# Fp32 transformer block on one core: low parts of w2 subtracted on GpSimd in most of the first phase, and a new order of the opening

## The chip, the cores and the metric

The kernel runs on one core of one Trainium2 chip. The metric is the device time of one execution in microseconds (us), lower is better. A run's time is compared with that of the kernel before.

## The reference

The input x has 2048 tokens of 576 values, all in fp32. The output is the sum of x, a local attention and a relu MLP, both fed with the same normalised x:

```python
xn = (x - mean(x)) / sqrt(var(x) + 1e-5)            # by token
q, k, v = split(xn @ wqkv)                          # 32 heads of 18
# each token sees itself and 7 earlier ones: offsets 0, 2, 4, ... 14
logits = einsum("bhsd,bhswd->bhsw", q, kg) * 18**-0.5   # masked before the start
attn = softmax(logits)
A = einsum("bhsw,bhswd->bhsd", attn, vg) @ wo       # wo 576 x 576
B = maximum(xn @ w1, 0) @ w2                        # 576 -> 4608 -> 576
out = x + A + B
```

## The kernel before

**Split in two.** Each fp32 operand of a matmul is held as a high part (rounded to the short form fp32r) and a low part (the rest), and a product is made of three: high x high, high x low, low x high. `hi_lo` makes the parts: ACT rounds (L395), then DVE subtracts (L398) or, with `by_pool`, GpSimd does (L401; GpSimd is called POOL). The products with w1 and wqkv are regrouped as in Strassen's method into seven products, P1 to P7, each 7 matmuls into one bank of PSUM (`bk`, `bkA`, `pm`); sums of weights (`ts`, `wset`) and of x (`xs`) are formed by DVE, and partial results are carried in the tiles `sn`, to which DVE adds a bank (`sn<-bk`, L398). Only then may PE write that bank again.

**Phases, sets, groups.** The offsets are even, so even and odd tokens are independent: the kernel does the 1024 even ones, then the odd ones, in two phases. A phase goes through 25 sets of weights: 18 F sets (256 of the 4608 hidden values each, numbered m = 0 to 17 and 18 to 35) and 7 Q sets (256 columns of wqkv). For an F set the hidden values go to `hb` (ACT's relu and a low part by DVE, L819), and are multiplied with that group's 256 rows of w2, tiles `w2t`, two of 128x576 a group, into the two accumulators `po`. `w2_make` fetches w2 from a copy that GpSimd's DMAs (L588, each behind a one-element copy L587 that paces it) have made in the order of use (`w2c`, in the first phase; the other weights have such copies too), and splits it.

**Attention.** Four units a phase, 8 heads each, on DVE: for 8 blocks of tokens products q x k (L1299) and their sums (L1302), a mask by GpSimd (L1305), the softmax (L1311 to L1326), products with v (L1331) and three levels of sums (L1338), then a transpose of the result (L1344). SP, the queue of most DMAs, writes it out (L1351, L1359); for the last unit of a phase it reads back 16 columns of each head group (L1365), which DVE transposes (L1369, `turn16`). Group 17's output product with wo needs all that; L786 and L791 load the rows of wo for it.

**What sets the order.** A planner, class `Order`, runs while the program is written out. It keeps a clock for each engine, queues of operations with due times and estimated durations, and `back`, a list of DVE operations of the attention (added by `later`) that fill DVE's gaps. An operation takes its place in its engine's stream when the planner's clock says that it is ready and nothing more urgent is. An engine then runs its stream strictly in order. At group 16 of a phase all that is left in `back` is forced out (`wo_plan`).

**The opening.** The list `OPEN` gives PE's order until the seven-product form starts: T transposes of x, R its last 64 rows, F and Q products with the first F set and the first Q set (Q001: the first with the Q set), O products with w2, K starts of copies, B, W, S, M others. Ahead of it stand loads: x of the first blocks in `x_first`, the first sets in the order `RAWS`, whose four members C11 to C22 are 256 rows by 128 columns and whose member `None` is the last 64 rows. `normalise` of a block is: statistics (`bn_stats`, L433), mean and variance (`bn_aggr`, L440, L441) on DVE, the root on GpSimd (L442, L445), and the scaling by ACT (L453, with `by_act`) or DVE (L458). Before the opening PE runs warm-up matmuls (L385).

Of the kernel before, what the change touches and what calls it, by code (L numbers as in the profile page):

```python
# [31 lines left out]
WARM = 38  # L32
PADS = (16, 16, 32, 32)
OPEN = """
T2 K2 B0 W0 R2 B1 T3 Q001 R3 Q000 T4 F010 F011 R4 T5 O0101 R5 O0100 T6 K3
Q011 S0 R6 O0110 F100 T7 O0111 Q010 R7 S1 F101 O1000 F110 K4 F111 O1010
Q100 M2 O1001 O1011 W1 Q111 O1100 O1101 O1111 O1110 Q110 Q101
""".split()

S2, S4, S3, S1 = range(4)  # L40
T1, B11, T3, B21, B22, T2, T4 = range(7)
B12 = T3
C11, C12, C21, C22 = range(4)
ROWS = (0, 288)
R3 = 96
# [3 lines left out]
FAR = 1e9  # L49
# [15 lines left out]
class Order:  # L65
# [120 lines left out]
        return op  # L186

    def later(self, fn, n, after=(), lag=0.0):
        op = Op(DVE, n / 960.0 + 0.068, fn, after, FAR, lag)
        self.back.append(op)  # L190
        return op

# [60 lines left out]
def tile_body(ctx: ExitStack, tc: tile.TileContext, x, wqkv, wo, w1, w2, out):  # L253
# [172 lines left out]
    def normalise(i, src, after, slack, by_act=False, alloc=True):  # L426

        z = {}

        def sums():  # L430
            z["st"] = smp.tile([P, 2, 6], F32, name="bst", bufs=4)
            for h in range(2):
                nc.vector.bn_stats(z["st"][:, h, :], src()[:, h * D2 : (h + 1) * D2])  # L433

        def rest():
            v = MV[0]
            MV.append(MV.pop(0))
            z["mv"] = mv = v[:, 0:2]
            z["r"] = r = v[:, 2:3]
            nc.vector.bn_aggr(mv, z["st"])  # L440
            nc.vector.tensor_scalar(mv[:, 1:2], mv[:, 1:2], EPS, None, op0=ALU.add)  # L441
            nc.gpsimd.tensor_tensor(r, mv[:, 1:2], mhalf, op=ALU.pow)  # L442
            if by_act:
                z["nm"] = nm = v[:, 3:4]
                nc.gpsimd.tensor_scalar(nm, mv[:, 0:1], r, -1.0, op0=ALU.mult, op1=ALU.mult)  # L445

        a = dve(sums, D + 200, after, slack)
        b = dve(rest, 310, [a], slack + 0.5, lag=1.1 if by_act else 0.8)

        def one():  # L450
            if alloc:
                xn_alloc(i)
            nc.scalar.activation(XN[i], src(), AF.Identity, bias=z["nm"], scale=z["r"])  # L453

        def two():
            if alloc:
                xn_alloc(i)
            nc.vector.tensor_scalar(XN[i], src(), z["mv"][:, 0:1], z["r"], op0=ALU.subtract, op1=ALU.mult)  # L458

        def fours():  # L460
            src = XN[i].rearrange("p (q c) -> p q c", q=2)[:, :, 2 * P : 2 * P + DH]
            nc.gpsimd.tensor_copy(XF[0][:, i % 2], src[:, :, None, :].to_broadcast([P, 2, 4, DH]))

        if by_act:
            MEANS[i] = b
            a = act(one, D + 200, [b], slack + 1.0)
        else:
            a = dve(two, D // 2 + 100, [b], slack + 1.0)
        NORMED[i] = a
        before, XUSED[i] = XFREE[i % 2], stub()  # L470
        XFREE[i % 2] = XUSED[i]
        FOURS[i] = o_.gp(fours, 256, [a, before], slack + 2.0)

    FOURS, XF, XUSED, XFREE = {}, [None], {}, [None, None]

# [295 lines left out]
    def w2_make(m, f, after=()):  # L771
        W2[m, f] = w = w2p.tile([P, 2, D], F32R, name="w2t")
        g = send(lambda: nc.sync.dma_start(f32(w[:, 1]), W2C[m % NP][f * P : (f + 1) * P]), 295, [*kept["w2", m % NP], *after], 4.0)
        W2OK[m, f] = hi_lo(w[:, 0], w[:, 1], f32(w[:, 1]), D, [g], (7 if SETS[SF[m] - 1][1] == "Q" else 24 if NP <= m < NP + 3 else 12) + 2 * f)

    WO, WOOK = {}, {}

# [814 lines left out]
        XLAST[i] = max(HALVES[i], key=lambda z: z.end)  # L1592
    ST0 = [stp[b].tile([P, 2, 2, P], F32, name=f"stg{b}") for b in range(3)]
    nc.gpsimd.memset(ST0[2][R3:P], 0.0)
    RAWS = ((C11, 0, 0), (C21, 1, 0), (C12, 0, 1), (C22, 1, 1), (None, 0, 0))
    def by_pool_now(fn, kb):
        fn()
        o_.clk[GP_] += 0.6
        z = Op(GP_, 0.0, None, (), 0.0)
        z.end = o_.clk[GP_] + 2.4 + kb / 60.0  # L1600
        o_.dma += kb / 300.0
        return z

    STOF = {C11: ST0[0][:, 0], C21: ST0[0][:, 1], C12: ST0[1][:, 0], C22: ST0[1][:, 1]}
    SETOK[0], SETREST = {}, {}
    first = []
    for s_, hf, f in RAWS:
        if s_ is None:
            got = [
                by_pool_now(lambda: nc.gpsimd.dma_start(  # L1610
                    ST0[2][y * DH : (y + 1) * DH].rearrange("p v f c -> p v (f c)"),
                    last_rows(w1[:, 0 : 2 * P])), 64)
                for y in range(3)
            ]
        else:
            got = [send(lambda: nc.sync.dma_start(
                STOF[s_], w1[ROWS[hf] : ROWS[hf] + 256, f * P : (f + 1) * P].rearrange("(k p) c -> p k c", p=P)), 128)]
        first.append((s_, got))
# [46 lines left out]
    fours_home()  # L1665
    o_.clk[PE] = 7.5
    normalise(0, lambda: X[0], [XLAST[0]], 0, by_act=True)
    normalise(1, lambda: X[1], [XLAST[1]], 1)
    def norm1():
        NORM1.end = NORMED[1].end  # L1670

# [11 lines left out]
    for z, (s_, got) in enumerate(first):  # L1683
        after, behind = [*got, NORMED[0] if z else None], [NORMED[1] if z else None]
        if s_ is None:
            first_rest(0, ST0[2].rearrange("p v f c -> p (v f) c"), after, 3 + z, behind)
        else:
            SETOK[0][s_] = hi_lo(
                wset(0)[0][:, s_, 0:2], wset(0)[1][:, s_], STOF[s_], 256, after, 3 + z, behind, z > 1,
            )  # L1690
    for z in SETOK[0].values():
        z += SETREST[0]
# [143 lines left out]
```

## Time and profile before

Three runs: 1115.68 to 1116.13 us, median 1115.89. The profiled execution:

| | us |
|---|---|
| time of that execution | 1115.5 |
| its span in the trace | 1113.7 |
| PE (TensorE) busy | 1095.4 (98%) |
| DVE (VectorE) busy | 916.1 (82%) |
| ACT (ScalarE) busy | 759.2 (68%) |
| POOL (GpSimd) busy | 214.9 (19%) |

PE is the matmul engine, PEld its weight loads; their clock is granted by a throttle (1.00 is full speed). A row of a group reads: line, engine, operation, output<-inputs, sizes, count | busy us in total, mean ns of one | idle time of the engine ahead of it, and what ended most of it. A row of a timeline reads: start, duration, engine, line, operation, names, sizes, count [idle ahead <- what ended it]. All times count from the span's start. Names are those of the tiles; `pr` and `qo` are the attention's products and results, `xa`, `xr` the normalised x and its last rows.

### The profile page before, as it was taken

The numbers are of one execution on the slowest core, as the hardware profiler recorded it, in microseconds if no ns is written. First come the engines' busy times: TensorE is split into PE (matmuls) and PEld (weight loads), VectorE is DVE, ScalarE is ACT, GpSimd is POOL, SyncE is SP. The second block draws the span as 40 slices with busy tenths as digits, with TensorE's granted clock in tenths as the row PEclk, the third lists the DMA queues.
The fourth block names the chain that finished last, engine by engine and source line by source line (L and its number), as shares of the span: only waits on it lengthen the run. The fifth ranks groups of instructions, "written<-read, shape, count | busy, mean of one in ns | idle before, by whom it ended". The sixth has DMA issues, their size and how long they took to land.

```text
span 1113.7 us, 23965 instructions
## 1 busy us (share of the span) xinstructions
PE 1095.4 (98%) x8971; PEld 1091.8 (98%) x8971; DVE 916.1 (82%) x1722; ACT 759.2 (68%) x1575; POOL 214.9 (19%) x427
## 2 busy tenths in 40 slices
PE   7999999999999999979999999999999999999998
PEld 7999999999999999979999999999999999999998
DVE  6966999998999889975795689998999998997540
ACT  6856676567777767756695655666567776766774
POOL 6232473332752253310220000000000000000000
PEclk9999999999999999999999999999999999999999
DMA  6689788884894455345363864646535416223312
GB/s 187 191 203 218 182 204 236 214 212 135 257 229 130 124 153 168 105 96 141 109 183 83 205 145 91 160 112 138 140 104 139 123 44 158 84 63 74 104 51 85
DMA packets 357012, 160.93 MB, mean 144 GB/s; under 512 B 211200, under 2 KB 335552, under 8 KB 355664
## 3 DMA queue, kind: packets, MB, share of 16 engines
q1 hardware_dynamic: 349392, 135.81, 48.0%
q0 software_dynamic: 7344, 23.29, 7.1%
q8 instruction: 70, 1.15, 0.4%
q10 hardware_dynamic: 160, 0.30, 0.1%
q14 instruction: 46, 0.38, 0.1%
HBM read 126.62 MB, written 55.41 MB: 163 GB/s over the span
## 4 chain that ended last, share of the span: by engine, by line
PE 86%; DVE 6%; DMA 3%; ACT 2%; SPq 1%; issue 1%; POOL 0%; DVEq 0%; ACTq 0%; POOLq 0%
PE po L404 41%; PE bk L404 26%; PE pm L404 12%; PE bkA L404 6%; DMA x<-in_x 1%; DVE pr L1338 1%; DVE xa L398 1%; DMA kk<-qd 1%; DVE wset L398 1%; DVE pr L1331 1%; DVE xs L398 1%; SPq L859 1%; DVE hb L819 0%; DVE ts L398 0%; DMA qo<-in_w 0%
## 5 line engine op out<-in xcount | busy, mean ns | idle before, releaser
L404 PE MATMUL po<-w2t,hb 128*128 128x256 f32 (+1 forms) x3456 | 504.4, 292 | 0.0
L404 PEld LDWEIGHTS po<-w2t,hb 128*128 128x128 f32 x3456 | 463.6, 188 | 0.3 <-DVE hb L819 0.3
L395 ACT ACTIVATE x<-po 128x576 f32<-128x576 f32 x286 | 186.3, 651 | 224.3 <-PE po L404 223.5
L404 PE MATMUL bk<-xs,wset 128*128 128x256 f32 (+1 forms) x1584 | 222.4, 277 | 0.3 <-ACT bkA L395 0.2
L404 PEld LDWEIGHTS bk<-xs,wset 128*128 128x128 f32 (+1 forms) x1584 | 202.6, 186 | 0.8 <-ACT bkA L395 0.4
L404 PE MATMUL bk<-xa,wset 128*128 128x256 f32 (+1 forms) x1116 | 193.5, 279 | 6.5 <-DVE sn L398 6.4
L395 ACT ACTIVATE po<-x 128x576 f32<-128x576 f32 x286 | 187.1, 655 | 6.0 <-DVE x L398 0.2
L404 PEld LDWEIGHTS bk<-xa,wset 128*128 128x128 f32 (+1 forms) x1116 | 159.6, 188 | 7.4 <-DVE sn L398 7.1
L587 POOL COPY spare<-hb 1x1 f32<-1x1 f32 x175 | 87.8, 501 | 236.4 <-ACT hb L395 236.1
L404 PE MATMUL pm<-xs,wset 128*128 128x256 f32 (+1 forms) x720 | 102.0, 277 | 0.0
L404 PE MATMUL pm<-xa,wset 128*128 128x256 f32 (+1 forms) x552 | 94.5, 278 | 1.7 <-POOL wset L401 1.2
L404 PEld LDWEIGHTS pm<-xs,wset 128*128 128x128 f32 (+1 forms) x720 | 92.0, 187 | 0.1
L398 DVE TENSOR_TENSOR sn<-bk,sn 128x256 f32<-128x256 f32 (+1 forms) x132 | 55.0, 418 | 44.2 <-PE bk L404 21.9
L404 PE MATMUL bkA<-xa,wset 128*128 128x256 f32 (+1 forms) x636 | 89.8, 278 | 0.0
L1305 POOL TENSOR_SCALAR_AFFINE_SELECT lg<-lg 1x512 f32<-1x512 f32 x8 | 9.8, 1224 | 411.3 <-DVE lg L1302 411.3
L1299 DVE TENSOR_TENSOR pr<-qo,kk 128x1152 f32<-128x1152 f32 x64 | 85.2, 1344 | 3.7 <-DMA qo<-qd 3.4
L1302 DVE TENSOR_REDUCE lg<-pr 128x64 f32<-128x1152 f32 x64 | 85.3, 1342 | 0.4
L1331 DVE TENSOR_TENSOR pr<-lg,v 128x1152 f32<-128x1152 f32 x64 | 85.4, 1348 | 0.1
L395 ACT ACTIVATE hb<-sn 128x256 fp32r<-128x256 f32 x140 | 57.6, 414 | 39.8 <-DVE sn L398 39.0
L404 PEld LDWEIGHTS bkA<-xa,wset 128*128 128x128 f32 (+1 forms) x636 | 82.9, 187 | 0.2 <-ACT bkA L395 0.2
L404 PEld LDWEIGHTS pm<-xa,wset 128*128 128x128 f32 (+1 forms) x552 | 77.8, 187 | 2.3 <-POOL wset L401 1.6
L1338 DVE TENSOR_TENSOR pr<-pr 128x288 f32<-128x288 f32 (+1 forms) x128 | 70.8, 599 | 0.0
(162 smaller groups left out, 1480.2 us busy)
## 6 DMA issues: line engine op xcount, KB each, us to landing
w2t<-w2c SPq DMA_DIRECT2D x70, 288.0 KB, 3.6
wset<-rwd SPq DMA_DIRECT2D x48, 336.0 KB, 4.1
qd<-stg SPq DMA_DIRECT2D x216, 64.0 KB, 2.6
wset<-w1c SPq DMA_DIRECT2D x105, 128.0 KB, 2.9
w2c<-in_w POOLq DMA_DIRECT2D x68, 144.0 KB, 3.7
rwd<-kk SPq DMA_DIRECT2D x18, 448.0 KB, 4.4
w1c<-in_w POOLq DMA_DIRECT2D x51, 128.0 KB, 3.9
out<-x SPq DMA_DIRECT2D x16, 288.0 KB, 2.2
```

The source lines that it names most:

```text
L395: nc.scalar.activation(o, i, func)
L398: nc.vector.tensor_tensor(o, a, b, op=op)
L404: nc.tensor.matmul(o, l, r, start=start, stop=stop, skip_group_check=True)
L587: nc.gpsimd.tensor_copy(spare[0:1], f32(LATEST[-1])[0:1, 0:1])
L859: lambda: nc.sync.dma_start(dst.rearrange("i (b r) c -> r (i b) c", r=32), z[32 * a : 32 * (a + 1)].rearrange("r j (z c) -> r (j z) c", c=32),
L1299: nc.vector.tensor_tensor(pr[i], q, window(k, i), op=ALU.mult)
L1302: nc.vector.tensor_reduce(s["lg"][:, i], pr.pop(i).rearrange(heads, d=Dh), axis=AX.X, op=ALU.add)
L1305: nc.gpsimd.affine_select(out=z, in_=z, pattern=[[1, NI], [1, W], [0, HG]], compare_op=ALU.is_ge, fill=-1e9 / scale, base=1 - W, channel_m ...
L1331: nc.vector.tensor_tensor(pr[i].rearrange(heads, d=Dh), e, window(VV[u % 2], i).rearrange(heads, d=Dh), op=ALU.mult)
L1338: nc.vector.tensor_tensor(o, z[:, 0:n], z[:, n : 2 * n], op=ALU.add)
```

## The change

- `w2_make` gives `by_pool` for m = 2 to 15: 28 subtractions of 128x576 go from DVE (L398) to GpSimd (L401).
- `RAWS` has the last rows second, and their three loads are issued by SP instead of GpSimd (`by_pool_now` is gone). C12 and C22 of the first set keep their low parts on GpSimd (`z > 2`).
- `TOLD` lets the second x's statistics start only after the first x's mean is formed.
- The planner's estimates: a `later` operation of more than 500 elements is taken as 0.042 us longer, GpSimd's copy `fours` as 110 elements instead of 256.
- `OPEN` has a new order.

```diff
-T2 K2 B0 W0 R2 B1 T3 Q001 R3 Q000 T4 F010 F011 R4 T5 O0101 R5 O0100 T6 K3
-Q011 S0 R6 O0110 F100 T7 O0111 Q010 R7 S1 F101 O1000 F110 K4 F111 O1010
-Q100 M2 O1001 O1011 W1 Q111 O1100 O1101 O1111 O1110 Q110 Q101
+B0 K2 T2 B1 W0 R2 K3 T3 Q001 R3 Q000 T4 F011 F010 Q011 R4 T5 R5 O0100 O0101
+K4 O0110 F101 S0 T6 F100 Q010 T7 R6 R7 O0111 S1 O1000 O1010 F111 F110 Q100
+M2 O1001 O1011 O1100 Q111 W1 O1110 O1101 O1111 Q110 Q101
...
     def later(self, fn, n, after=(), lag=0.0):
-        op = Op(DVE, n / 960.0 + 0.068, fn, after, FAR, lag)
+        op = Op(DVE, n / 960.0 + (0.11 if n > 500 else 0.068), fn, after, FAR, lag)
...
-        FOURS[i] = o_.gp(fours, 256, [a, before], slack + 2.0)
+        FOURS[i] = o_.gp(fours, 110, [a, before], slack + 2.0)
...
-        W2OK[m, f] = hi_lo(w[:, 0], w[:, 1], f32(w[:, 1]), D, [g], (7 if SETS[SF[m] - 1][1] == "Q" else 24 if NP <= m < NP + 3 else 12) + 2 * f)
+        W2OK[m, f] = hi_lo(w[:, 0], w[:, 1], f32(w[:, 1]), D, [g], (7 if SETS[SF[m] - 1][1] == "Q" else 24 if NP <= m < NP + 3 else 12) + 2 * f, by_pool=2 <= m < NP - 2)
...
-    RAWS = ((C11, 0, 0), (C21, 1, 0), (C12, 0, 1), (C22, 1, 1), (None, 0, 0))
-    def by_pool_now(fn, kb):
...
+    RAWS = ((C11, 0, 0), (None, 0, 0), (C21, 1, 0), (C12, 0, 1), (C22, 1, 1))
...
-                by_pool_now(lambda: nc.gpsimd.dma_start(
+                send(lambda: nc.sync.dma_start(
                     ST0[2][y * DH : (y + 1) * DH].rearrange("p v f c -> p v (f c)"),
                     last_rows(w1[:, 0 : 2 * P])), 64)
...
-    normalise(1, lambda: X[1], [XLAST[1]], 1)
+    TOLD = Op(DVE, 0.0, None, [MEANS[0]], 0.0)
+
+    def told():
+        TOLD.end = MEANS[0].end - MEANS[0].lag
+
+    MEANS[0].post = told
+    normalise(1, lambda: X[1], [XLAST[1], TOLD], 1)
...
-                wset(0)[0][:, s_, 0:2], wset(0)[1][:, s_], STOF[s_], 256, after, 3 + z, behind, z > 1,
+                wset(0)[0][:, s_, 0:2], wset(0)[1][:, s_], STOF[s_], 256, after, 3 + z, behind, z > 2,
```

After the opening PE's instructions stand in the same order in both kernels. Three places show what moves on the other engines. First DVE at the end of the first phase's last attention unit (`qo_...` its result), before:

```order
L1338 TENSOR_TENSOR pr<-pr 128x576 x2
L1338 TENSOR_TENSOR pr<-pr 128x288 x2
L1338 TENSOR_TENSOR qo_5631<-pr 128x144 x2
L1344 STREAM_TRANSPOSE pr<-qo_5631 128x1024
L1369 STREAM_TRANSPOSE pr<-pr 128x512
L398 TENSOR_TENSOR sn_152<-bk_156,sn_152 128x256
L398 TENSOR_TENSOR sn_153<-bk_158,sn_153 128x256
L819 SCALAR_TENSOR_TENSOR hb_141<-bkA,hb_141 128x256
L398 TENSOR_TENSOR w2t<-w2t 128x576
```

and the same place now:

```order
L1338 TENSOR_TENSOR qo_5644<-pr 128x144 x2
L1344 STREAM_TRANSPOSE pr<-qo_5644 128x1024
L398 TENSOR_TENSOR sn_152<-bk_156,sn_152 128x256
L819 SCALAR_TENSOR_TENSOR hb_142<-bkA,hb_142 128x256
L398 TENSOR_TENSOR w2t<-w2t 128x576
L819 SCALAR_TENSOR_TENSOR hb_143<-sn_152,hb_143 128x256
L1369 STREAM_TRANSPOSE pr<-pr 128x512
L398 TENSOR_TENSOR sn_153<-bk_158,sn_153 128x256
```

L1369 stood directly behind L1344, ahead of two `sn` additions; now four instructions, the first `sn` addition among them, stand between.

Second, GpSimd's stream early in the first phase, where the two low parts of group 2 now stand (copies of w2, then of wqkv, around them):

```order
L587 COPY spare<-hb_144 1x1
L588 DMA w2c_219<-in_w 16x2304
L401 TENSOR_TENSOR w2t<-w2t 128x576 x2
L587 COPY spare<-hb_141 1x1
L588 DMA w2c_219<-in_w 16x2304
L587 COPY spare<-hb_143 1x1
L588 DMA w2c_219<-in_w 16x2304
```

Before, the pacing copies and DMAs followed each other without the subtractions; the last two parts of this copy of w2 now stand behind them.

Third, DVE in the opening, ahead of the four subtractions for the first Q set (`wset_136<-kk,wset_136 128x256 x4`) and behind the second hidden low part (`hb_142<-pm`), before:

```order
L819 SCALAR_TENSOR_TENSOR hb_142<-pm,hb_142 128x256
L433 BN_STATS bst<-x_122 128x6 x2
L398 TENSOR_TENSOR wset_136<-kk,wset_136 128x256 x4
L398 TENSOR_TENSOR xa_127<-bk_158,xa_127 128x4x128
L440 BN_AGGR mv_147<-bst 128x2
```

and now:

```order
L819 SCALAR_TENSOR_TENSOR hb_142<-pm,hb_142 128x256
L440 BN_AGGR mv_140<-bst 128x2
L441 TENSOR_SCALAR mv_140<-mv_140 128x1
L433 BN_STATS bst<-x_122 128x6 x2
L440 BN_AGGR mv_147<-bst 128x2
L441 TENSOR_SCALAR mv_147<-mv_147 128x1
L398 TENSOR_TENSOR wset_136<-kk,wset_136 128x256 x4
```

Two means stand ahead of the four subtractions where none stood.

More of the change, by code (lines that the diff above doesn't have):

```diff
@@ L1594, in tile_body @@
     nc.gpsimd.memset(ST0[2][R3:P], 0.0)
-    RAWS = ((C11, 0, 0), (C21, 1, 0), (C12, 0, 1), (C22, 1, 1), (None, 0, 0))
-    def by_pool_now(fn, kb):
[L1597 to L1602, printed above, removed]
+    RAWS = ((C11, 0, 0), (None, 0, 0), (C21, 1, 0), (C12, 0, 1), (C22, 1, 1))
     STOF = {C11: ST0[0][:, 0], C21: ST0[0][:, 1], C12: ST0[1][:, 0], C22: ST0[1][:, 1]}
```

## Prediction

> **What bounds the kernel now.** I read the page first: TensorE (PE) is busy 1095.4 us of a span of 1113.7, so only some 18 us can be won without fewer matmuls, and the change has the same matmuls. The next view is what PE waited for, longest first:
>
> ```profile
> PE bk L404 <- DVE sn L398: 6.4, 1, 6.4
> ...
> PE bk L484 <- ACT pr L453: 1.9, 1, 1.9
> ...
> PE pm L404 <- POOL wset L401: 1.2, 2, 1.0
> ```
>
> One wait of 6.4 us outweighs all the others. Stretches of the span tell where it lies and what came with it (columns: stretch, length, busy time of PE, PE's weight loads, DVE, ACT, POOL with instruction counts, granted clock, DMA share, GB/s):
>
> ```profile
> 20.00:72.00 52.00, 51.54 (x431) 51.06 (x430) 49.19 (x114) 38.70 (x82) 11.36 (x26) 1.00 0.60 152
> 72.00:480.00 408.00, 407.43 (x3360) 406.75 (x3359) 363.99 (x656) 281.91 (x585) 170.37 (x344) 1.00 0.69 185
> 480.00:494.33 14.33, 14.33 (x117) 14.10 (x115) 12.98 (x22) 9.08 (x18) 0.00 (x0) 1.00 0.21 51
> 494.33:500.74 6.41, 0.00 (x2) 0.00 (x1) 1.08 (x3) 0.65 (x1) 0.00 (x0) 0.77 0.88 189
> ...
> 496.00:498.00 2.00, 0.00 (x0) 0.00 (x0) 0.00 (x0) 0.00 (x0) 0.00 (x0) 0.94 0.98 160
> 500.74:504.00 3.26, 3.26 (x15) 3.26 (x16) 2.94 (x7) 1.65 (x4) 0.00 (x0) 0.50 0.63 127
> ```
>
> PE is full before and after; it is empty from 494.33 to 500.74, the end of the first phase's last attention unit. DVE is 364 of 408 us busy up to there and 12.98 of 14.33 just ahead. The chain of waits through the hole (start, length, what):
>
> ```profile
> 491.77 1.26 DVE pr L1344
> ...
> 495.81 0.78 SPq L1365
> ...
> 496.63 3.66 DMA qo<-woc
> ...
> 500.74 3.35 PE bk L404 x14
> 504.09 1.87 PE po L404 x12
> ```
>
> and the instructions at its end and just ahead of it, from the timeline:
>
> ```profile
> 491.81 0.85 PE L404 MATMUL bk<-xs,wset 128*128 128x256 f32 x6
> 492.61 1.72 PE L404 MATMUL po<-w2t,hb 128*128 128x256 f32 x12
> ...
> 499.66 0.71 DVE L1369 STREAM_TRANSPOSE pr<-pr 128x512 f32<-128x512 f32 x1 [6.65 <-DMA pr<-o]
> 500.30 0.72 DVE L398 TENSOR_TENSOR sn<-bk,sn 128x256 f32<-128x256 f32 x2
> 500.74 0.58 PE L404 MATMUL bk<-xa,wset 128*128 128x256 f32 x1 [6.41 <-DVE sn L398]
> ```
>
> DVE finishes the unit with the transpose L1344 at 491.77, SP sends the result out and reads 16 columns a head group back (L1365), and the transpose of these, L1369, can start only at 499.66: 7.89 us after L1344. DVE takes its instructions in order, the two additions `sn<-bk` stand behind L1369, and PE's next set needs the banks they read. The hole costs more than its 6.41 us. The clock is 0.94 on average over 496 to 498, which puts its fall to one half near 497.8, some 3.4 us after PE stopped, and PE starts again at half clock: 14 matmuls into bk and 12 into po take 5.22 us (500.74 to 505.96). Just before, seven of the first kind took 0.80 (491.81 to 492.61, one row between not shown) and twelve of the second 1.72, so 3.32 for as many. That is 1.90 lost; hole and clock together 8.3.
>
> **The low parts of w2.** 28 subtractions go from DVE to GpSimd (POOL). What DVE pays now, over the first phase and in the last unit's window, and one subtraction with its successors:
>
> ```profile
> L398 DVE TENSOR_TENSOR w2t<-w2t 128x576 fp32r<-128x576 f32 x28 | 20.9, 753 | 1.2 <-ACT w2t L395 0.8
> ...
> L398 DVE TENSOR_TENSOR w2t<-w2t 128x576 fp32r<-128x576 f32 x6 | 4.4, 754 | 0.4 <-ACT w2t L395 0.4
> ...
> 405.38 1.19 SPq L1253 DMA_DIRECT2D qo<-qd  x2
> ...
> 409.45 1.32 DVE L1299 TENSOR_TENSOR pr<-qo,kk 128x1152 f32<-128x1152 f32 x1
> ...
> 177.55 0.75 DVE L398 TENSOR_TENSOR w2t<-w2t 128x576 fp32r<-128x576 f32 x1
> 178.22 0.30 DVE L1338 TENSOR_TENSOR qo<-pr 128x144 f32<-128x144 f32 x1
> ...
> 181.59 1.58 PE L404 MATMUL po<-w2t,hb 128*128 128x256 f32 x11
> ```
>
> One takes 0.75 us but the next instruction starts after 0.67, so six give 4.0. I count only these six for L1344: the last unit's first product (L1299 at 409.45) needs the fetch that SP issues at 405.38, when PE has got far enough for it, and starts 4.1 later, so what earlier units win ends in a wait for that fetch. By the time alone L1344 would fall to 487.8. On POOL one costs twice as much, and it is not without effect on DVE:
>
> ```profile
> 17.74 1.42 POOL L401 TENSOR_TENSOR w2t<-qo,w2t 128x576 fp32r<-128x576 f32 x1
> ...
> 20.97 1.35 POOL L401 TENSOR_TENSOR wset<-kk,wset 32x512 fp32r<-32x512 f32 x1
> 21.09 1.51 DVE L398 TENSOR_TENSOR wset<-kk,wset 128x256 fp32r<-128x256 f32 x1
> ...
> L398 DVE TENSOR_TENSOR wset<-wset 128x256 fp32r<-128x256 f32 x17 | 7.1, 420 | 1.0 <-ACT wset L395 0.5
> ...
> 470.18 6.05 POOL L587 COPY spare<-hb 1x1 f32<-1x1 f32 x1
> ```
>
> The DVE subtraction of 128x256 that started 0.12 us behind POOL's took 1.51 instead of 0.42: it ended 0.28 after POOL's end, as if it had waited for it. The other way round, a POOL copy of one element took 6.05 us beside DVE's products and sums of the attention. So each of the six costs DVE between 0 (POOL comes into a gap, or meets an instruction that takes one operand from a bank) and 1.1 us: L1344 between 487.8 and 494.3. I take one full collision, 1.1, because four of the six fall where reductions (which read one operand) alternate with the products, and only the last pair in the stretch of products and sums: L1344 at 488.9. The Trainium skill, page "SBUF — State Buffer", section "SBUF: two separate sides", says that DVE and GpSimd share a port pair under an exclusive lock, which a DVE instruction with two SBUF operands takes against a GpSimd one that reads SBUF, and that the loser blocks for the whole instruction; the 1.51 agrees. By that rule alone each low would cost DVE up to its 1.42 against the 0.67 saved, and the change would lose: that is the third rival.
>
> The 7.89 us from L1344 to L1369 hold transfers and SP only and stay: L1369 at 496.8. The order of DVE changes there too: one `sn<-bk` addition now comes ahead of L1369 and one behind. PE therefore goes on past 494.33 by the half set that the first frees, 0.80, to 495.1; the second is done 0.64 (499.66 to 500.30) and 0.44 (500.30 to 500.74) after L1369's start, at 497.9. **A hole of 2.8 us is left, below the 3.4 after which the clock fell.** The terms: -6.41 - 1.90 + 2.8 = -5.5. The hole's bounds are 1.7 (no collision) and about 8 (six).
>
> **PE waiting for POOL's lows.** The low of w2 is now two POOL instructions of 1.42 behind ACT's rounding, and with DVE's products around them they can starve. In the rows above PE used at 181.59 a w2 whose first low DVE did at 177.55; POOL, from the same start, would end the second at 180.4 undisturbed. In groups 2 to 6 I find such margins of 1 to 4 us, later 11 or more. POOL's own queue hides nothing there, but what stands behind the pair are copies of weights for the second phase, not needed before 500. Bounds: 0, and some 3 if three of five groups come 1 us late. I take +1.0, the nearest row being that margin of 1.
>
> **The opening.** The new order of loads and DVE work concerns these rows:
>
> ```profile
> 4.38 0.82 DVE L433 BATCH_NORM_STATS2 bst<-x 128x6 f32<-128x288 f32 x2 [4.38 <-DMA x<-in_x]
> 6.86 0.82 DVE L433 BATCH_NORM_STATS2 bst<-x 128x6 f32<-128x288 f32 x2 [1.66 <-DMA x<-in_x]
> ...
> 7.60 0.19 DVE L440 BATCH_NORM_AGGREGATE mv<-bst 128x2 f32<-128x12 f32 x1
> ...
> 7.89 0.20 DVE L440 BATCH_NORM_AGGREGATE mv<-bst 128x2 f32<-128x12 f32 x1
> ...
> 9.10 0.87 ACT L453 ACTIVATE pr<-x,mv 128x576 f32<-128x576 f32 x1 [1.58 <-POOL mv L445]
> ...
> 19.02 0.42 DVE L819 SCALAR_TENSOR_TENSOR hb<-pm,hb 128x256 fp32r<-128x256 f32 x1 [0.69 <-ACT hb L395]
> 19.36 0.81 DVE L433 BATCH_NORM_STATS2 bst<-x 128x6 f32<-128x288 f32 x2
> 20.09 2.51 DVE L398 TENSOR_TENSOR wset<-kk,wset 128x256 fp32r<-128x256 f32 x4
> ...
> 22.64 0.60 PE L404 MATMUL pm<-xa,wset 128*128 128x256 f32 x3
> ```
>
> The first x's mean waits from 5.20 to 7.60 behind the second's statistics, whose data come at 6.86. With it put ahead, ACT's normalisation comes about 1.6 us earlier (POOL's steps, 1.5, then follow 5.5; the first weights' rounding takes ACT to 7.5), and the first transposes with it. Three loads go from POOL's queue to SP's ahead of three 128-KB loads; the queue is full then, so these come later by what 192 KB take, below 1 us. The chain ends, however, at 22.64: PE there wants the four lows of 20.09, and between the hidden low (19.02) and these DVE now has two means beside the pair of statistics (19.36) that stood there; a mean takes 0.3 (7.60 to 7.89). The hidden low, which follows the first normalisation through two steps of PE, comes perhaps 1.4 earlier, DVE's work is 0.6 longer, the loads come later: between 0 and 0.8 earlier in all. PE is full from there (51.54 of 52). I take the middle, -0.4; bounds -1.5 (all of the first advance) and +2 (loads late by 1 and a collision with POOL of 1.1).
>
> The planner's changed estimates (0.11 for long DVE steps, 110 for GpSimd's copies) move instructions and cost nothing themselves; the orders show them.
>
> **Sum.** -5.5 + 1.0 - 0.4 = -4.9 against the profiled execution's 1115.5, which is 0.4 under the median of 1115.89: the forecast for the median is 1111.0.
>
> **Rivals.**
> First, *no collision*: POOL finds gaps. L1344 at 487.8, hole 1.7, small waits 0: -6.41 - 1.90 + 1.7 - 0.4 = -7.0, or 1108.9; with the opening's -1.5, 1107.8. For it: DVE's bank reads and reductions between; against: the 6.05 shows few gaps.
> Second, *the clock falls again*: two collisions make the hole 3.9, past 3.4, and the 1.90 come back: 2.0 less to win than in the forecast by clock, 1.1 by the hole, so -1.9 and 1114.0. The Trainium skill, page "TensorE: Matmul & The Clock Gate", section "Why this matters for your kernels", would have no gap above about 3 us; a hole of 3.0 to 3.4 would by that already pay the 1.90.
> Third, slower, *the lock costs more than the move saves*: from 0.67 per low on, DVE is later than before. If all six wait a full 1.1, L1344 is at 494.3, L1369 at 502.2, PE starts at 503.3: a hole of 8.2 with the half clock, 1.8 more than before, and 1.0 to 3 of small waits in the 408 us where DVE has 44 idle: +3.5 with a middle 2.1 and the opening's -0.4, 1119.4. For it: the pair of 1.35 and 1.51; against: reductions and bank reads are half of DVE's work.
> Fourth, *PE waits for POOL's lows group by group*: five groups late by 1.2 each, as the starved copy allows, give back 6 of the 5.9: 1116.
>
> **Chances.** Forecast 0.45, first 0.17, second 0.12, third 0.12, fourth 0.14. A measurement of this kernel tells 0.2% (2.2 us) from nothing. Faster: 0.45 + 0.17 + 0.06 of the second (1114.0 lies just at the bound) = 0.68; slower: the third, 0.12; the same: 0.20. The range, 1107.0 to 1117.0, holds the first in most of its width and the fourth, and leaves out the third; the forecast's own is 1109 to 1113.
>
> **What would show it.** Right: PE's longest wait between 1.5 and 3.4 us near 495, again for an `sn` addition, behind a L1369 that waits for its read-back; the clock 1.00 from 490 to 506; L1344 2 to 4 us earlier; no w2 low among PE's waits above 1 us; Q001's matmuls (22.64) within half a us. A DVE product of over 2 us beside a POOL low shows a collision. Wrong would be: L1344 unmoved (DVE not the limit there), PE waits `po <- POOL w2t L401` in several groups, or a hole above 3.5 with clock 0.50 behind it.

## The result and the profile after

The changed kernel takes 1122.38 us (median of 4 runs, 1120.77 to 1122.90) against 1116.01 for the kernel before (4 runs): a ratio of 1.0052, 95% interval 1.0034 to 1.0069. By that ratio it is 5.8 us slower (the medians lie 6.4 apart). The profiled execution was the slowest of the four, 1122.90, and its span grew by 7.1, from 1113.7 to 1120.8; what follows is read from it. What PE waits for now, longest first:

```profile
PE bk L404 <- DVE sn L398: 7.0, 4, 4.1
PE pm L404 <- DVE sn L398: 2.5, 3, 1.3
PE pm L404 <- POOL wset L401: 2.3, 2, 1.6
PE bk L404 <- ACT bkA L395: 1.8, 1, 1.8
```

The one wait of 6.4 has become one of 4.1, and six others for `sn` additions have joined it. Stretches of the changed kernel:

```profile
12.00:16.00 4.00, 1.75 (x12) 1.19 (x10) 3.04 (x8) 2.97 (x7) 3.41 (x7) 0.90 1.04 354
16.00:20.00 4.00, 3.93 (x17) 3.91 (x18) 2.31 (x10) 1.93 (x5) 2.82 (x6) 0.50 0.97 203
20.00:24.00 4.00, 4.00 (x26) 4.00 (x25) 2.39 (x6) 1.95 (x5) 2.60 (x4) 0.74 0.02 4
72.00:480.00 408.00, 401.25 (x3296) 399.33 (x3295) 362.34 (x615) 274.73 (x572) 212.54 (x364) 1.00 0.69 182
505.04:509.15 4.11, 0.00 (x1) 0.00 (x1) 1.08 (x3) 0.00 (x0) 0.00 (x0) 1.00 0.82 214
509.15:516.00 6.85, 6.85 (x43) 6.85 (x44) 2.39 (x5) 5.08 (x11) 0.00 (x0) 0.75 0.41 83
```

Between 72 and 480 PE is idle for 6.75 us where it was idle for 0.57. DVE is as busy there as before (362.3 against 364.0) although the 28 subtractions, 20.9 us, are gone from it. The opening has nearly seven microseconds at half clock (means of 0.90, 0.50 and 0.74 over its three stretches of 4 us), and the hole still ends with some (0.75 over 6.85 us, 1.7 lost).

PE's instructions stand in the same order in both kernels, so the start of one matmul in both gives the lead or lag at that place. Here and below a lag is that of PE against the profiled execution of the kernel before. The first row is of the kernel before, the rows after it of the changed one (timelines):

```profile
111.86 1.72 PE L404 MATMUL po<-w2t,hb 128*128 128x256 f32 x12
```

```profile
114.15 1.72 PE L404 MATMUL po<-w2t,hb 128*128 128x256 f32 x12
...
499.98 1.25 DVE L1344 STREAM_TRANSPOSE pr<-qo 128x1024 f32<-128x1024 f32 x1
...
501.71 0.85 PE L404 MATMUL bk<-xs,wset 128*128 128x256 f32 x6
...
508.07 0.71 DVE L1369 STREAM_TRANSPOSE pr<-pr 128x512 f32<-128x512 f32 x1 [5.21 <-DMA pr<-o]
508.71 0.39 DVE L398 TENSOR_TENSOR sn<-bk,sn 128x256 f32<-128x256 f32 x1
509.15 0.97 PE L404 MATMUL bk<-xa,wset 128*128 128x256 f32 x6 [4.11 <-DVE sn L398]
```

The lag is 2.3 us at 114 (2.5 at 74), and 9.9 just ahead of the hole: the matmuls that stood at 491.81 stand at 501.71. Behind the hole it is 7.4, and it stays there to the end (7.3). So: opening +2.5, stretch of 74 to 480 +7.4, hole -2.5.

### The profile page after: what moved, and what is told of

Its sections match the earlier page's. It is cut to its first block, busy times and chain, and to the rows that moved or that the text cites. A ratio compares the mean times of both kernels' runs of the same rounds, so it can differ in the third digit from the quotient of the medians.

```text
span 1120.8 us, 23979 instructions
## 1 busy us (share of the span) xinstructions
PE 1099.4 (98%) x8971; PEld 1093.8 (98%) x8971; DVE 919.8 (82%) x1694; ACT 757.9 (68%) x1575; POOL 269.3 (24%) x452
## 4 chain that ended last, share of the span: by engine, by line
PE 82%; DVE 11%; ACT 2%; issue 2%; DMA 1%; SPq 1%; POOL 0%; DVEq 0%; ACTq 0%; POOLq 0%
PE po L404 39%; PE bk L404 25%; PE pm L404 11%; PE bkA L404 6%; DVE pr L1331 2%; DVE pr L1338 2%; DVE hb L819 1%; DVE sn L398 1%; DVE kk L398 1%; DVE wset L398 1%; DVE qo L1338 0%; DVE pr L1299 0%; SPq L699 0%; DMA wset<-w1c 0%; DVE ts L398 0%
## 5 line engine op out<-in xcount | busy, mean ns | idle before, releaser
L587 POOL COPY spare<-hb 1x1 f32<-1x1 f32 x175 | 98.0, 560 | 120.4 <-ACT hb L395 120.0
L1299 DVE TENSOR_TENSOR pr<-qo,kk 128x1152 f32<-128x1152 f32 x64 | 93.0, 1463 | 3.7 <-DMA qo<-qd 3.5
L398 DVE TENSOR_TENSOR sn<-bk,sn 128x256 f32<-128x256 f32 (+1 forms) x132 | 55.2, 418 | 45.2 <-ACT hb L395 25.4
L1331 DVE TENSOR_TENSOR pr<-lg,v 128x1152 f32<-128x1152 f32 x64 | 89.7, 1416 | 0.2
L1338 DVE TENSOR_TENSOR pr<-pr 128x288 f32<-128x288 f32 (+1 forms) x128 | 75.2, 625 | 0.0
```

The costliest lines, as they stand in the source:

```text
L398: nc.vector.tensor_tensor(o, a, b, op=op)
L587: nc.gpsimd.tensor_copy(spare[0:1], f32(LATEST[-1])[0:1, 0:1])
L1299: nc.vector.tensor_tensor(pr[i], q, window(k, i), op=ALU.mult)
L1331: nc.vector.tensor_tensor(pr[i].rearrange(heads, d=Dh), e, window(VV[u % 2], i).rearrange(heads, d=Dh), op=ALU.mult)
L1338: nc.vector.tensor_tensor(o, z[:, 0:n], z[:, n : 2 * n], op=ALU.add)
```

## The experiments

Each run is compared with the kernel before on the same chip, whose median was 1117.4 to 1118.0 there (1116.01 for the first row). The profiled execution of the kernel before, which the lags count from, took 1115.5, some 2 us less than these medians, so a lag at the end of a run can be 2 us larger than the loss that its ratio shows. In some of the profiles PE's idle time ahead of the first transposes was near 3 us instead of 2, with half clock behind it; at 72 these were 0 to 1 us late, and another (the lows of groups 13 to 15 alone) was 1.5 late with the clock at 1.00. A difference of that size there is not read as the work of an edit.

| run | ratio to before | 95% interval |
|---|---|---|
| changed kernel | 1.0052 | 1.0034 to 1.0069 |
| lows alone | 0.9982 | 0.9973 to 0.9991 |
| opening alone | 1.0015 | 1.0005 to 1.0024 |
| planner's figures alone | 1.0128 | 1.0107 to 1.0150 |
| changed kernel without the lows | 1.0111 | 1.0096 to 1.0126 |
| changed kernel with the old figures | 1.0002 | 0.9991 to 1.0013 |
| lows of groups 13 to 15 alone | 0.9976 | 0.9962 to 0.9990 |
| figure lower (0.03) | 0.9953 | 0.9937 to 0.9970 |
| 28 added GpSimd instructions, first | 1.0163 | 1.0148 to 1.0179 |
| 28 added GpSimd instructions, second | 1.0071 | 1.0056 to 1.0086 |
| opening alone, PE kept busy | 1.0010 | 0.9999 to 1.0020 |
| turn16 behind | 0.9961 | 0.9950 to 0.9972 |
| turn16 and wo behind | 0.9941 | 0.9922 to 0.9960 |

**The three parts.** My first theory, "lock", was that GpSimd's low parts hold up DVE, and that the waits between 140 and 400 come from that; its rival, "order", that they come from the planner's other order. The low parts alone:

```diff
-... else 12) + 2 * f)
+... else 12) + 2 * f, by_pool=2 <= m < NP - 2)
```

> The kernel before with one edit: the low parts of w2 of groups 2 to 15 by GpSimd; opening and planner figures as before. Theory 'lock': a GpSimd low holds up DVE's instructions with two SBUF operands for its whole 1.4 us, in pairs 2.8 us; DVE's products and subtractions that overlap a low are longer by some 0.9 us per low in all (25 us over 28 lows, against 19 saved), additions to sn behind them come late, and PE waits 1 to 2 us for an sn addition at three to five of the groups between 140 and 400 us, 5 to 7 us in all; opening as before. The hole at the end of the phase is 2 to 4 us smaller. Time 1117 to 1121. Theory 'order': the stalls of the changed kernel come from the planner's other order of DVE, not from the low parts on GpSimd: PE waits between 140 and 400 stay below 2 us in all here, time 1109 to 1114.

It took 1115.29 us, 0.18% less than before, which lies between the ranges of the two theories. The stretch of 72 to 480 has PE 402.75 us busy (5.3 idle), as "lock" had it; but the hole is not smaller, it is gone:

```profile
72.00:480.00 408.00, 402.75 (x3302) 400.47 (x3302) 364.71 (x633) 274.04 (x572) 201.16 (x364) 1.00 0.69 182
480.00:520.00 40.00, 40.00 (x330) 40.00 (x329) 20.38 (x46) 30.52 (x68) 2.49 (x8) 1.00 0.57 152
```

The lag rises to 7.1 us by 475, and the whole 8.5 of the hole come back. L1344 comes at 476.47, where PE is 7.1 late: against PE's work it is 22 us earlier than before. DVE's saved time doesn't account for that: 28 times 0.67 is 18.8 saved, and DVE's instructions that overlap a low are longer by 15.5. The order moved as well: the second unit's product with wo starts at 359.9 instead of 378.5, and SP issues the last unit's fetch (L1253) at 387.69 instead of 405.38.

The changed kernel without that part:

```diff
-... else 12) + 2 * f, by_pool=2 <= m < NP - 2)
+... else 12) + 2 * f)
```

> The changed kernel with one edit: all low parts of w2 on DVE again; the opening and the planner's figures as changed. Theory 'lock': no PE wait above 0.7 us between 140 and 480, the hole near 495 is back at 5.5 to 6.5 us with half clock behind it, the opening costs 1 to 2.5 us: 1116.5 to 1118.5. Theory 'order': the 5 to 7 us of waits between 140 and 400 remain and the hole is back as well: 1122 to 1126.

Neither theory had this: 1129.61. The middle is clean (407.83 of 408 busy) and the opening costs 0.4 to 1 us, but the hole is 10.2 us, with a second one of 5.7. So I ran the planner's figures by themselves:

```diff
-        op = Op(DVE, n / 960.0 + 0.068, fn, after, FAR, lag)
+        op = Op(DVE, n / 960.0 + (0.11 if n > 500 else 0.068), fn, after, FAR, lag)
...
-        FOURS[i] = o_.gp(fours, 256, [a, before], slack + 2.0)
+        FOURS[i] = o_.gp(fours, 110, [a, before], slack + 2.0)
```

> The kernel before with the planner's two changed figures alone (0.11 for long DVE steps of the attention, 110 for the copies on GpSimd). DVE's order has L1369 behind one sn addition instead of ahead of two. Theory 'lock': no new waits in 72 to 480, hole shorter by 0.8, time 1115.2 (1114.5 to 1116.5). Theory 'order': PE waits of 1 to 2 us for sn additions appear at some groups between 140 and 400, time 1119 to 1122.

They cost 1.28%, 14 us. The groups of DVE's attention work between 72 and 480, before and with the figures alone:

```profile
L1331 DVE TENSOR_TENSOR pr<-lg,v 128x1152 f32<-128x1152 f32 x28 | 37.4, 1345 | 0.0
L1338 DVE TENSOR_TENSOR pr<-pr 128x576 f32<-128x576 f32 (+1 forms) x56 | 30.9, 599 | 0.0
```

```profile
L1331 DVE TENSOR_TENSOR pr<-lg,v 128x1152 f32<-128x1152 f32 x24 | 32.0, 1352 | 0.1
L1338 DVE TENSOR_TENSOR pr<-pr 128x576 f32<-128x576 f32 (+1 forms) x48 | 27.0, 600 | 0.0
```

and the end of the last unit with the figures alone:

```profile
501.46 1.25 DVE L1344 STREAM_TRANSPOSE pr<-qo 128x1024 f32<-128x1024 f32 x1
502.63 0.39 DVE L398 TENSOR_TENSOR sn<-bk,sn 128x256 f32<-128x256 f32 x1
...
503.07 1.65 PE L404 MATMUL bk<-xa,wset 128*128 128x256 f32 x6 [10.19 <-DVE sn L398]
...
509.37 0.71 DVE L1369 STREAM_TRANSPOSE pr<-pr 128x512 f32<-128x512 f32 x1 [6.36 <-DMA pr<-o]
510.01 0.39 DVE L398 TENSOR_TENSOR sn<-bk,sn 128x256 f32<-128x256 f32 x1
...
510.45 1.65 PE L404 MATMUL bk<-xa,wset 128*128 128x256 f32 x6 [5.52 <-DVE sn L398]
```

With 0.11 the planner takes DVE's long steps as 0.042 longer than before and lets it do fewer of them in the gaps: by 480 four products and eight of the larger sums fewer, and four of the smallest (not shown), 10 us of DVE's work in all. The two figures were changed together here; that 0.11 does it, and not the 110, is argued from these missing steps and from the next run, not shown by a run of its own. All that is left is forced out in one piece at group 16, ahead of the next `sn` addition, and PE stands for it (10.2), then again for L1369 (5.5), with the clock at a mean of 0.74 over 480 to 520.

That the figure works through how early the attention is done, I tested by turning it the other way, on the kernel before:

```diff
-        op = Op(DVE, n / 960.0 + 0.068, fn, after, FAR, lag)
+        op = Op(DVE, n / 960.0 + (0.03 if n > 500 else 0.068), fn, after, FAR, lag)
```

> The kernel before with the planner's figure for DVE's long attention steps at 0.03 instead of 0.068 (the change has 0.11). If the figure works by how early the planner lets DVE do attention work, DVE does 5 to 10 us more of it before 480 than before, L1344 comes 3 us or more earlier against PE, the hole is 2 to 4 us: 3 to 6 below before, less what new waits of 1 us for late sn additions cost in both phases. If the cost of 0.11 was a chance of one order, this one is as likely worse: within 2 us of before or above.

0.47% faster, 5.3 us, within what I expected if the figure works that way. L1344 came at 489.12, where PE was 0.7 late, 3.4 earlier than before against PE; no new waits in the first phase up to 480 (407.69 busy); the wait that is left is 2.6. DVE's busy time up to 480 rose by only 1.6 us, less than the 5 to 10 that I had expected; the rest of the lead lies in what it did there.

The changed kernel with both old figures:

```diff
-        op = Op(DVE, n / 960.0 + (0.11 if n > 500 else 0.068), fn, after, FAR, lag)
+        op = Op(DVE, n / 960.0 + 0.068, fn, after, FAR, lag)
...
-        FOURS[i] = o_.gp(fours, 110, [a, before], slack + 2.0)
+        FOURS[i] = o_.gp(fours, 256, [a, before], slack + 2.0)
```

> The changed kernel with the planner's two figures as before (0.068 and 256): low parts on GpSimd and the new opening. If the figures, which alone cost 12 us at the hole, cost the changed kernel its gain: the hole of 495 to 510 is gone as in the kernel with the low parts alone, the waits of 140 to 400 (7 us) stay, the opening adds 0 to 2.5: 1 to 3 us below before to 1 above, some 6 us under the changed kernel. If the figures cost nothing here, the hole of 4 us with its half clock stays, and the time is that of the changed kernel.

1117.99, a ratio of 1.0002. The hole is gone (40.00 of 40 busy from 480 to 520), the middle as with the lows alone (403.02 of 408). So the figures cost the changed kernel 0.5%, some 5.6 us, all of it at the hole.

And the opening's changes alone, which is the same edit with the low parts back on DVE as well (`RAWS`, the three loads by SP, `TOLD`, `z > 2` and `OPEN` are what is left of the change):

```diff
-... else 12) + 2 * f, by_pool=2 <= m < NP - 2)
+... else 12) + 2 * f)
```

> The kernel before with the opening's changes alone (rows second and by SP, first mean ahead, new order of the opening). The first transposes 2 us earlier, then PE waits 1.6 and 0.7 us for GpSimd's low parts (C12, C22). If the clock falls there, as in the changed kernel's profile (0.50 from 16 to 20), PE is 0.9 later near 23 us and 2 or more near 72: time +1 to +3 against before. If it doesn't fall, PE is 0 to 0.6 ahead at 23 and within 1 us at 72: time -0.5 to +1.

+0.15%, 1.7 us; in its profile the lag is 0.3 at 23 and 3.4 at 71, and the clock 0.69 from 16 to 20. Most of the lag thus arises behind 23: from 24 to 72 PE is busy 45.27 of 48 us, where it was 47.54.

The lows and the opening add up (0.9982 x 1.0015 = 0.9997, measured 1.0002). The figures do not: 14 us by themselves, 5.6 with the lows.

**The cost of a GpSimd low part by itself.** To separate DVE's delay from its new order, I left all low parts on DVE and gave GpSimd 28 instructions that change no value:

```diff
+        if 2 <= m < NP - 2:
+            z = o_.gp(lambda: nc.gpsimd.tensor_tensor(w[:, 0], f32(w[:, 0]), one.to_broadcast([P, D]), op=ALU.mult), D, W2OK[m, f], 12)
+            W2OK[m, f] = [*W2OK[m, f], z]
```

> The kernel before, all low parts of w2 on DVE, with 28 added GpSimd instructions: at groups 2 to 15 GpSimd multiplies each high part of w2 (128x576) by one in place, so the values stay as they are. DVE's stream keeps its instructions and nearly its order. Theory 'lock': the added GpSimd instructions, 1.4 us each, hold up DVE's instructions with two SBUF operands by 0.9 us each on average, 25 us in all with nothing saved; PE waits for sn additions in several groups between 100 and 480, 10 us or more in all, and the last unit ends later: time 1125 to 1140. Theory 'order' (the waits of 140 to 400 come from DVE's new order once the low parts are gone): no waits above 1 us there, time within 2 us of before.

1136.77, but PE was slower all the time, in the second phase too, where there are none of these instructions; the run says nothing of the lock. The second attempt keeps the constant in the unused tile `pad1`, so that nothing moves in memory:

```diff
-    one = keep.tile([P, 1], F32, name="one")
-    nc.gpsimd.memset(one, 1.0)
+    nc.gpsimd.memset(pad1[:, 0:1], 1.0)
...
-            z = o_.gp(lambda: nc.gpsimd.tensor_tensor(w[:, 0], f32(w[:, 0]), one.to_broadcast([P, D]), op=ALU.mult), D, W2OK[m, f], 12)
+            z = o_.gp(lambda: nc.gpsimd.tensor_tensor(w[:, 0], f32(w[:, 0]), pad1[:, 0:1].to_broadcast([P, D]), op=ALU.mult), D, W2OK[m, f], 12)
```

> As the run with 28 added GpSimd instructions, but the constant lies in a tile that was there already, so that no other tile changes its place in memory (in the first such run the added tile moved the others by 4 bytes, and PE's matmuls ran slower over the whole span, which hides the rest). Theory 'lock': DVE's instructions that overlap the added ones are longer by 15 to 25 us in all, PE waits 3 to 8 us more for sn additions between 72 and 480, and the last unit ends later, so that the hole grows: before + 5 to + 15 us. Theory 'order': before within 2 us.

+0.71%, 7.9 us. PE's idle time between 72 and 480 rose from 0.57 to 3.6 (404.37 busy), the lag by 6.2, and the hole to 8.2. DVE's instructions that overlap the 28 (38.7 us of GpSimd) are longer than the median of their kind by 18.7 us, 0.67 each. With nothing saved and nearly the same order of DVE, the 7.9 us are what these added instructions cost. As a price of the lows the 18.7 is rough: some 5 of it fall on DVE's own subtractions of w2 (mean 925 ns against 753), which the changed kernel no longer has there.

**Fewer lows.** The six that I had counted for L1344, on the kernel before:

```diff
-... else 12) + 2 * f)
+... else 12) + 2 * f, by_pool=13 <= m < NP - 2)
```

> The kernel before with the low parts of w2 of groups 13 to 15 alone on GpSimd, the six that fall into the last unit of the first phase; DVE has L1369 behind one sn addition. Theory 'lock': up to 400 us no new waits (offset to before below 0.5), then some 1 to 2 us of waits at the three pairs; L1344 earlier against PE by 0 to 2 us, the hole 3.5 to 5.5 us and the clock down again: 1113 to 1117. If the lock cost nothing, L1344 would be 4 us earlier and the hole 1.6: 1108 to 1110.

-0.24%. No new waits up to 440 beyond one of 1.0 at 194 that lies in the loads; L1344 at 492.52 with PE 2.9 late, so 2.2 earlier against PE, and a hole of 4.3 with half clock. It is the lateness of PE that makes it earlier: by the time alone L1344 came 0.75 later, and 1.5 of PE's 2.9 were there at 74, long ahead of the first of these lows at 418.9.

**The opening's clock.** 14 transposes of the identity in PE's first wait:

```diff
+            if last and f == 1:
+                keep_warm(14, bk3)
             t = pe(f_, (4 + 2 * last) * 0.1135, after)
```

> The kernel with the opening's changes alone, with 14 transposes of the identity (1.5 us of PE) added in PE's first wait for GpSimd's low part near 13 us; they compute nothing that is used. If the loss of the opening is the half clock behind these two waits, the clock stays at 1.00 from 12 to 24, PE is 0.5 to 1.5 us earlier near 23 us than in the opening alone, and the time falls by 1 to 2 us against it. If the loss lies in the order behind (PE's wait of 2.1 for a hidden low part near 40), the time stays within 0.7.

The waits, and the clock over 12 to 16, 16 to 20 and 20 to 24, in the opening alone and with the transposes:

```profile
15.42 0.51 PE L404 MATMUL pm<-xa,wset 128*128 128x256 f32 x2 [1.62 <-POOL wset L401]
16.62 0.50 PE L404 MATMUL pm<-xa,wset 128*128 128x256 f32 x2 [0.69 <-POOL wset L401]
...
12.00:16.00 4.00, 2.30 (x16) 1.75 (x15) 3.04 (x8) 3.63 (x9) 3.52 (x7) 1.00 1.09 353
16.00:20.00 4.00, 3.38 (x17) 3.36 (x18) 2.79 (x11) 1.82 (x5) 3.32 (x6) 0.69 1.06 235
20.00:24.00 4.00, 4.00 (x32) 4.00 (x31) 3.21 (x10) 2.58 (x5) 2.71 (x5) 0.89 0.01 2
```

```profile
12.00:16.00 4.00, 3.51 (x27) 2.92 (x26) 2.97 (x9) 3.56 (x8) 3.38 (x6) 1.00 1.08 344
16.00:20.00 4.00, 3.70 (x29) 3.70 (x30) 2.79 (x12) 2.55 (x6) 3.31 (x6) 1.00 1.02 229
20.00:24.00 4.00, 3.79 (x32) 3.55 (x31) 3.80 (x11) 3.32 (x8) 3.51 (x7) 1.00 0.07 16
```

The clock stays at 1.00, and PE comes to the first product with the Q set 1.9 us earlier (21.05 against 22.93). At 71 only 1.0 of that is left, as the start of one matmul shows in the kernel before, in the opening alone and with the transposes:

```profile
70.99 0.84 PE L404 MATMUL bk<-xs,wset 128*128 128x256 f32 x6
```

```profile
74.41 0.84 PE L404 MATMUL bk<-xs,wset 128*128 128x256 f32 x6
```

```profile
73.38 0.84 PE L404 MATMUL bk<-xs,wset 128*128 128x256 f32 x6
```

The lag there is 2.4 instead of 3.4. The waits behind the half clock are in both: 2.0 for a hidden low part near 40 (2.1 in the opening alone), and near 70 waits that add 1.4 to the lag (1.0). So the clock is worth about 1 us of the opening's lag at most, no more than profiles differ there anyway, and the larger part lies in the waits behind it; no run takes these out. The time is 1118.12 against 1119.34, 1.2 us less, but the intervals of the two ratios overlap, so the run's time doesn't show the gain. Its profiled execution, the slowest of its ten, also had a wait of 2.8 at 194 for a late load, which the edit doesn't touch.

**Taking the hole out directly.** L1369 is placed by the planner when it takes the read-back as landed. 4 us more there:

```diff
-                got.end = send(lambda: nc.sync.dma_start(s["o16"], O16), 262, [o16]).end
+                got.end = send(lambda: nc.sync.dma_start(s["o16"], O16), 262, [o16]).end + 4.0
```

> The kernel before with one edit: the planner takes the read-back of the 16 columns (L1365) as landing 4 us later, so that L1369 stands behind both sn additions and the five instructions after them. If the hole at 494 to 501 is nothing but L1369 standing ahead of these additions, PE has no wait above 1 us there, the clock stays at 1.00, and the time falls by the 8.3 us of hole and clock: 1107 to 1109. If something else of the chain (the second output of L1351, the rows of wo) ends last, a wait of 3 us or more moves to 505 to 530, and the time is 1111 to 1116.

-0.39%. The wait of 6.4 became one of 3.3, now for a low part of `hb` behind L1369: as in the other branch of what I expected, but the thing that waits is DVE's order again. The profile also had a wait of 2.5 at 193 for a late load, which with the clock behind it added 3.5 us to the lag and lies far ahead of the place that the edit moves. So in the next I gave the read-back 12 us, and let the rows of wo and the attention's output tiles count as landing 7 us later, so that their low parts, too, come behind the `sn` additions:

```diff
-... O16), 262, [o16]).end
+... O16), 262, [o16]).end + 12.0
...
-... *turned[ph, u], OQ[ph, u]], 3.0))
+... *turned[ph, u], OQ[ph, u]], 10.0 if u == NU - 1 else 3.0))
...
-... [*kept["wo",], *VDONE], 3.0,
+... [*kept["wo",], *VDONE], 10.0,
...
-... 2.5 if u < NU - 1 else 1.2)]
+... 2.5 if u < NU - 1 else 8.0)]
```

> The kernel before with the planner told that the read-back of L1365 lands 12 us later, the rows of wo for the last unit 7 us later and the attention's output tiles for it 7 us later, so that L1369 and the low parts of wo stand behind all sn additions that PE wants first. No other change. If nothing but DVE's order makes the hole, PE has no wait above 1 us between 490 and 530, the clock stays at 1.00: 7 to 8.5 us below before. If the chain through the read-back sets the end all the same, a wait of 3 us or more shows at the product with wo: 2 to 5 below before.

1111.05 us, -0.59% (interval 0.40 to 0.78), 6.6 us faster than the kernel before, a little less than the 7 to 8.5 that I expected, and by the ratios 1.1% faster than the changed one. Its stretch:

```profile
480.00:520.00 40.00, 39.05 (x315) 38.59 (x314) 27.19 (x55) 27.77 (x59) 0.00 (x0) 1.00 0.50 124
```

One microsecond of idle time is left and the clock holds. L1344 stands where it stood (491.85); L1369 runs at 506.14, and nothing waits for it.

## Why the prediction was wrong, by its steps

The forecast was 4.9 us faster; the time is 5.8 us slower, on the side of the third rival but not by its path: that rival had the hole grow to 8.2, and it shrank to 4.1. Term by term, in the profile, the hole gave -2.5 where I had -5.5, the waits +7.4 where I had +1.0, the opening +2.5 where I had -0.4. Two steps failed by about 6 us each.

**The planner's figures: "cost nothing themselves".** The first of the two. I had no reason for this zero. I read the new order only at the few instructions behind L1344, and took its place from the old order less what six subtractions save. The figures alone push 10 us of the attention behind 480 and cost 14 us; in the changed kernel they cost 5.6 us, at the hole.

**"I count only these six for L1344."** In the changed kernel the reason held: the last unit's first product, at 418.89, stood idle 1.69 us for the fetch, which SP issued from 414.87. With the old figures it doesn't hold: there the fetch itself comes earlier, and L1344 is 22 us earlier against PE. In the changed kernel L1344, at 499.98 with PE 9.9 late, is 1.7 earlier against PE, where I had 2.9. The 7.89 from L1344 to L1369 was right (8.09), the half set ahead too (0.80). So the hole of 2.8 came out as 4.1, with half clock behind it (0.75 over 6.85 us): the second rival's case, and a sign that I had named as one of being wrong. The term of -5.5 was -2.5.

**The collisions.** The mechanism was named, in the third rival, the size not: I had one full collision of 1.1 among six, 0.18 a low. In the changed kernel the instructions of DVE that overlap a low are longer by 25.8 us over the 28, 0.92 each, against the 0.67 that each saves. The products of q and k show it in the mean of a group (72 to 480; it was 1346 ns before and is 1347 with the figures alone):

```profile
L1299 DVE TENSOR_TENSOR pr<-qo,kk 128x1152 f32<-128x1152 f32 x32 | 50.3, 1584 | 3.6 <-DMA qo<-qd 3.5
```

With the old figures it is 15.5 us, 0.55 each: less than the saving. So the third rival's condition, 0.67 per low, was passed in the one order and not in the other.

**"PE waiting for POOL's lows".** The second of the two steps, and the term with the largest miss. PE never waits for a low of w2; that fear, and with it the fourth rival, was groundless. But the term +1.0 that stood for it should have stood for another: +7.4. A pair of lows holds DVE up, and the `sn` addition in the queue behind is late (changed kernel):

```profile
214.39 3.03 POOL L401 TENSOR_TENSOR w2t<-w2t 128x576 fp32r<-128x576 f32 x2 [11.53 <-ACT w2t L395]
...
214.60 2.99 DVE L1338 TENSOR_TENSOR qo<-pr 128x144 f32<-128x144 f32 x2
217.62 1.25 DVE L1344 STREAM_TRANSPOSE pr<-qo 128x1024 f32<-128x1024 f32 x1
218.79 1.31 DVE L1299 TENSOR_TENSOR pr<-qo,kk 128x1152 f32<-128x1152 f32 x1
220.03 0.41 DVE L398 TENSOR_TENSOR sn<-bk,sn 128x256 f32<-128x256 f32 x1
...
220.50 0.95 PE L404 MATMUL bk<-xa,wset 128*128 128x256 f32 x6 [1.65 <-DVE sn L398]
```

Two sums that take 0.52 together elsewhere took 2.99, each ending 0.17 behind one of the two lows, and PE stood for 1.65. The Trainium skill, page "SBUF — State Buffer", section "SBUF: two separate sides", has the loser of the shared port pair blocked for the whole instruction. The trace agrees, with these two sums, and in three places of the changed kernel it goes further: there one DVE instruction waited out two lows in a row, though it had started ahead of them. A subtraction of kk, 0.29 elsewhere, took 3.47:

```profile
299.83 3.47 DVE L398 TENSOR_TENSOR kk<-kk 128x128 f32<-128x128 f32 x1
...
300.32 2.82 POOL L401 TENSOR_TENSOR w2t<-w2t 128x576 fp32r<-128x576 f32 x2
```

At 325.39 and 393.85 products of 1.35 took 4.68 and 4.56. With the low parts alone no DVE instruction lost as much (1.3 at most), so how a low collides hangs on DVE's order. I had weighed DVE's throughput and no latency: even where the lows save DVE time, PE stands for 5.3 us in the middle (lows alone) or 5.0 (old figures), where it stood for 0.57.

**The opening.** Forecast -0.4, bounds -1.5 to +2; measured +1.7 alone and +2.5 in the changed kernel's profile. The first normalisation came 2.2 us earlier, where I had worked out 1.6, and the four low parts ended at 20.97 instead of 22.60, better than I had it. What failed is "PE is full from there (51.54 of 52)". The first products now wait 1.62 and 0.70 for GpSimd's C12 and C22 (1.04 and 0.20 before), and the clock fell: twelve matmuls into po took 3.08 instead of 1.86. In the opening alone that leaves PE only 0.3 late at 23, and the lag then grows to 3.4 at 71, behind the place from which I took PE as full. With PE kept busy in the first wait it is still 2.4. The longest wait on the way is that of 2.1 for a hidden low part near 40; which part of the new order makes it, no run tells.

**The chances.** Slower had 0.12. The two cases that held most of the rest priced a lock and a hole, and none had the planner's order.

## What to carry to other kernels

Where a planner writes the order, a figure of its cost model is a change of the program: count how much background work it lets through before the point where the rest is forced, in the new order itself, over the whole stretch and not at its end. Moving an elementwise step to GpSimd is to be priced by what it does to the latency of the DVE instruction that PE waits for, not by DVE's busy time; here the dearest collisions were three in which one DVE instruction waited out a pair. A hole that one misplaced instruction makes is best removed by placing that instruction: four constants in the planner gained 6.6 us where the whole change lost 5.8.

## What the runs showed of the hardware that I had not expected

- The clock fell with less than 3 us of idle time. In the lower-figure run PE stood still for 2.61 us and the clock over the next four was 0.57; there it fell only after PE had started again, for the twelve matmuls at 499.40 took 2.99 instead of 1.72. In the changed kernel's opening one idle time of 1.62 was enough: the clock is 1.00 up to 15.23 and 0.50 from there, ahead of the second idle time of 0.70. The kernel before stood still for 1.95 us at 8.07 and kept 1.00. So the length of the idle time alone doesn't decide, and my margin "below the 3.4 after which the clock fell" was none. The Trainium skill, page "TensorE: Matmul & The Clock Gate", section "Why this matters for your kernels", puts the bound at gaps of about 3 us. Both 2.61 and 1.62 lie below it, and the measurement decides. The rows are of the lower-figure run, then of the changed kernel.

```profile
498.50 0.95 PE L404 MATMUL bk<-xa,wset 128*128 128x256 f32 x6 [2.61 <-DVE sn L398]
...
499.00:503.00 4.00, 4.00 (x22) 4.00 (x22) 1.62 (x4) 2.90 (x6) 0.00 (x0) 0.57 0.58 108
```

```profile
14.87:15.23 0.36, 0.36 (x2) 0.29 (x2) 0.36 (x1) 0.36 (x2) 0.36 (x1) 1.00 1.07 373
15.23:15.37 0.14, 0.14 (x2) 0.00 (x0) 0.14 (x2) 0.11 (x1) 0.14 (x1) 0.50 1.02 351
15.37:16.07 0.70, 0.00 (x0) 0.00 (x0) 0.70 (x3) 0.00 (x0) 0.70 (x2) 0.50 1.07 348
```

- A constant of 4 bytes a partition, put into a tile of its own, made PE 1.4% slower in a stretch where it was never idle: 3272 matmuls in 400 us against 3317 with the constant in an unused tile. The two programs differ only in that place; they ran on two chips, on which the kernel before took 1117.38 and 1117.67. The rows are of the first and the second run with added GpSimd instructions:

```profile
600.00:1000.00 400.00, 400.00 (x3272) 399.93 (x3271) 345.01 (x619) 264.48 (x550) 5.02 (x4) 1.00 0.51 120
```

```profile
600.00:1000.00 400.00, 400.00 (x3317) 399.87 (x3315) 350.14 (x626) 266.54 (x557) 5.02 (x4) 1.00 0.51 120
```

The 320-wide matmul into po took 310 ns there instead of 303. Which tile's place does it, no run tells.
